# P times V of a sliding-window attention in eight 64x32 array tiles instead of four 128x32 ones

## The chip, the cores and the metric

The kernel runs on one core of a Trainium2 chip. The metric is the time of one execution on the device in microseconds (us); smaller is better. Names of engines in the profile: PE is TensorE's matmul, PEld its weight load, DVE is VectorE, ACT is ScalarE, POOL is GpSimd, SP is SyncE, which here only issues transfers.

## The reference

One transformer block on 2048 tokens of width 640. The normalised input goes through attention (32 heads of 20, causal, each query sees the last 256 keys, itself included) and through a gated feed-forward part of width 1728; both are added to the input.

```python
def _A_ref(x, wqkv, wo):
    H = 32; Dh = D // H; W = 256
    qkv = (x @ wqkv).reshape(B, S, 3, H, Dh).transpose(2, 0, 3, 1, 4)
    q, k, v = qkv[0], qkv[1], qkv[2]
    scores = jnp.einsum("bhqd,bhkd->bhqk", q, k) * (Dh ** -0.5)
    mask = (idx[:, None] - idx[None, :] >= 0) & (idx[:, None] - idx[None, :] < W)
    p = _softmax(jnp.where(mask, scores, -1e9))
    o = jnp.einsum("bhqk,bhkd->bhqd", p, v)
    return o.transpose(0, 2, 1, 3).reshape(B, S, D) @ wo
def _B_ref(x, w_gate, w_up, w_down):
    return (_gelu(x @ w_gate) * (x @ w_up)) @ w_down
xn = _layernorm(x)
return x + _A_ref(xn, A_wqkv, A_wo) + _B_ref(xn, B_w_gate, B_w_up, B_w_down)
```

## The kernel before

There are four stages: normalisation and the first projections (to about 60 us of the profile), attention with dense matmuls as filler (about 60 to 575 us), the rest of the gate and up projections, and the down and output projections. The change lies in the second.

Attention works in units. Unit u is a group g of four heads and a chunk c of 512 queries (u = 4 g + c; 8 groups, 4 chunks, 32 units). For a unit the kernel makes, in this order over time:

- **Max tiles** (`max_pair`, matmuls in L522): scores of 128 queries for two heads against the keys of their window, in array tiles of 60 rows by 64 columns at row 0 or 64; the two heads go to two PSUM banks. VectorE reduces each bank to a maximum per query (L526; one reduction is an instruction and a read of its accumulator). Eight calls a unit make 16 banks. After the last, VectorE negates the maxima (L535, L536).
- **Score tiles** (`exp_piece`, L581): scores again, now keys by queries, one PSUM bank for each of 12 steps. ScalarE takes the exponential into the tile `P` (L583). There are three `P` tiles of 512 columns a unit, X, Z and Y (`pieces`): X holds key blocks b and b-2, Z holds b-1 and b+2, Y holds b+1 and b+3, where b = 4c is the chunk's first key block of 128 keys; a chunk with c = 0 has no earlier blocks. POOL then clears what the mask excludes (`clear`, L594 and L597), block by block in this order.
- **P times V** (`av_unit`, L608): for each piece of a key block (128 keys by n queries) and each of the four heads a matmul in float32, with the head's V (128 keys by 20, and a column of ones whose result is the softmax sum) as a stationary operand of 128 rows by 32 columns. The four heads lie in the four 32-column groups of the array, and all pieces add up in one PSUM bank, `ps_o`. One float32 matmul call shows as two records in the profile, and so does its weight load. ScalarE copies the bank to `ob` (L612), and SyncE's queue stores it (L616, L617).

All of these PSUM banks come from one ring of six (`bank`, L497): each allocation takes the next bank in turn, and its first matmul waits until the last reader of the bank's previous tile is done. Two further banks are for the dense filler.

The order on TensorE, VectorE, ScalarE and POOL is the order in which the program issues the instructions (a schedule written out by hand). `attention` issues a unit in 14 slots. In slot 0 it issues two `max_pair` calls (four banks), then `av_unit` of the unit before, then two more `max_pair` calls, then the first score tile; in slot 2 score tiles 1 to 4; in slots 4 and 8 two `max_pair` calls and two score tiles each; in slot 10 the last three score tiles. At the end of every slot come dense filler matmuls. These names are used below: e0 is the score tile of slot 0, e1 to e4 those of slot 2; max tiles 1 to 4 are the banks filled ahead of P times V in slot 0, and max tiles 5 to 8 those filled behind it.

Three helpers put work off. `defer(n, fn)` calls fn when slot `now + n` takes its list; a slot takes its list at its start, so what is deferred by 0 from within a slot is taken by the next one. `late(fn)` puts fn on a list that `flush` empties near the end of each slot, behind the score tiles; the negation of the maxima goes this way too.

```python
for i in range(NS):
    T = now[0] = NS * u + i
    for fn, a in tick():
        fn(*a)
    if i in BURSTS:
        pull_max(2, T)
    if i == 0 and u:
        av_unit(u - 1)
        flush()
        pull_max(2, T)
    for s in SCORES.get(i, ()) if u < NU else ():
        exp_piece(u, s)
    flush()
```

Of the kernel before, what the change touches and what calls it, by code (L numbers as in the profile page):

```python
# [12 lines left out]
AF = mybir.ActivationFunctionType  # L13
OP = mybir.AluOpType
# [5 lines left out]
C = 512  # L20
# [50 lines left out]
def block_kernel(ctx, tc, x, wqk, wv, wgu, wdo, wdl, out):  # L71
    nc = tc.nc
# [120 lines left out]
    done = set()  # L193
    now = [None]

    def at(slot, fn, *a):
        acts.setdefault(slot, []).append((fn, a))
# [31 lines left out]
    def defer(n, fn, *a):  # L229
        if now[0] is None:  # L230
            fn(*a)
        else:
            at(now[0] + n, fn, *a)
# [190 lines left out]
    with tc.tile_pool(name="lp", bufs=1, side="right") as lp:  # L424
# [5 lines left out]
        ps = psd.tile([128, C], F32, name="ps_u", tag="dn")  # L430
# [48 lines left out]
    vtiles = dict(enumerate(v0[2]))  # L479
# [17 lines left out]
    def bank(name):  # L497
        return psr.tile([128, C], F32, name=name, tag="ring")
# [49 lines left out]
    def pieces(c):  # L548
        b = 4 * c
        X = [(b, 0, 0, 384)] + ([(b - 2, 384, 0, 128)] if c else [])  # L550
        Y = [(b + 1, 0, 128, 384), (b + 3, 384, 384, 128)]
        Z = ([(b - 1, 0, 0, 256)] if c else []) + [(b + 2, 256, 256, 256)]
        return X, Z, Y
# [11 lines left out]
    pts = {}  # L565
# [21 lines left out]
    def clear(u, bi):  # L587
        c = u % NC
        pt = pts[u, bi]
        for p in pieces(c)[bi]:  # L590
            for col, diag in diag_tail(*p, c):
# [4 lines left out]
                else:  # L596
                    nc.gpsimd.affine_select(out=a, in_=a, pattern=[[0, 4], [-1, 128]], compare_op=OP.is_ge,  # L597
                                            fill=0.0, base=-1, channel_multiplier=1)

    def av_unit(u):  # L600
        g, c = divmod(u, NC)
        o, v = bank("ps_o"), vtiles[g]
        todo = [(pts[u, bi], *p) for bi, ps in enumerate(pieces(c)) for p in ps]
        for i, (pt, kb, col, q0, n) in enumerate(todo):
            assert (id(v), kb) in done, (u, kb)
            for j in range(4):
                w0_ = kb * 84 + 21 * j
                nc.tensor.matmul(o[32 * j:32 * j + 32, q0:q0 + n], v[:, w0_:w0_ + 32], pt[:, j, col:col + n],  # L608
                                 start=i == 0, stop=i == len(todo) - 1, skip_group_check=True,
                                 tile_position=(0, 32 * j))  # L610
        ob = ap.tile([128, C], F32, name="ob", tag="ob", bufs=1)
        nc.scalar.activation(ob, o, AF.Copy)  # L612

        def store():
            for j in range(4):
                nc.sync.dma_start(od[c].rearrange("(d h) t -> h d t", h=H)[4 * g + j], ob[32 * j:32 * j + DH, :])  # L616
            nc.sync.dma_start(sd[c][4 * g:4 * g + 4, :], ob[DH::32, :])  # L617

        defer(3, store)
# [184 lines left out]
    def attention():  # L804
# [18 lines left out]
        for u in range(NU + 1):  # L823
# [13 lines that stand above are left out]
                if i in POOL_SLOTS or T < NS:  # L837
                    release(2)
                if u + 3 < NU and i in (KSLOT, 12):
                    load_stack(u + 3, (int(i == KSLOT),))  # L840
                pull_fill(RATE / NS)
# [496 lines left out]
    for j, f in enumerate(range(NFA, NF - 1)):  # L1338
        end = f + 1 == NF - 1
        first, second = {i: [] for i in range(4)}, {i: [] for i in range(4)}  # L1340
# [91 lines left out]
    for n, (p, k) in enumerate(steps):  # L1432
        i = n % (NQD + 1)
        if i == 0:
            begun.clear()
            ps = {b: psn.tile([128, C], F32, name=f"ps_{b}", tag=f"b{b}") for b in (1, 2, 5, 3, 6, 4, 7, 8)}
# [71 lines left out]
```

## Time and profile before

| | us |
|---|---|
| median of 3 runs (1047.58 to 1047.95) | 1047.59 |
| span of the profiled execution, first to last instruction | 1046.8 |
| what lies around the span, against the median | 0.8 |
| TensorE busy (matmul) | 1035.2 |
| VectorE busy | 730.8 |
| ScalarE busy | 513.5 |
| P times V (L608): busy, in 1408 records | 84.3 |
| copy of `ps_o` (L612): 32 copies of 0.597 us | 19.1 |

A row of a group gives line, engine, operation, output and inputs, shapes, count, then busy time in us, the mean of one in ns, and after the second bar the idle time of that engine just before these instructions and what ended it. A row of the timeline gives start and duration in us, and for matmuls also the array tile (rows*columns) and the shape of the moving operand of the first in the run. A row of the windows gives the stretch, its length, the busy time of TensorE, its weight loads, VectorE, ScalarE and POOL with their counts, then the granted clock, the share of the DMA engines and GB/s. Matmuls are pipelined, so the time of a run is read from its start to the start of the next row, not from the durations.

### The profile page before, as it was taken

To read this page: it belongs to the slowest core of one execution; us is meant where nothing else is said; L and a number is where in the kernel's file an instruction comes from. 1 tells how busy PE (TensorE), PEld (TensorE's weight loads), DVE (VectorE), ACT (ScalarE), POOL (GpSimd) and SP (SyncE) were. 2 spreads that over 40 slices of the span, in tenths; PEclk is the share of its full clock that TensorE was granted. 3 is DMA by queue.
4 is the path that set the end of the run, shared out by engine and by line. 5 is a ranking of instruction groups with operands and counts; after the bars stand their busy time and mean duration, and the time that the engine had idled before them with its cause. 6 is when DMAs were issued, how large, how long until landed. Compare 5 with 4: busy or idle time off the path is not lost.

```text
span 1046.8 us, 22733 instructions
## 1 busy us (share of the span) xinstructions
PE 1035.2 (99%) x7997; PEld 827.6 (79%) x7997; DVE 730.8 (70%) x2007; ACT 513.5 (49%) x1088; POOL 333.8 (32%) x503
## 2 busy tenths in 40 slices
PE   8999999999999999999999999999999999999998
PEld 7987666666677766666666888888888999999998
DVE  8745656666665556677662677877655889888887
ACT  4444666765665566656565532223324554333332
POOL 5122667766464458474635111110110000000000
PEclk9999999999999999999999999999999999999999
DMA  5651465545332344444322557677217874443342
GB/s 200 189 150 59 135 183 159 179 148 180 96 117 72 111 145 144 139 130 130 112 79 75 191 189 244 213 251 253 100 61 250 270 241 137 134 128 113 125 134 94
DMA packets 105179, 158.56 MB, mean 151 GB/s; under 512 B 15420, under 2 KB 60092, under 8 KB 105064
## 3 DMA queue, kind: packets, MB, share of 16 engines
q1 hardware_dynamic: 102680, 150.95, 45.0%
q10 hardware_dynamic: 2384, 6.16, 1.9%
q8 instruction: 63, 1.03, 0.4%
q14 instruction: 52, 0.43, 0.1%
HBM read 101.78 MB, written 54.92 MB: 150 GB/s over the span
## 4 chain that ended last, share of the span: by engine, by line
PE 92%; DVE 3%; DMA 2%; ACT 1%; POOL 1%; issue 1%; SPq 0%; DVEq 0%; POOLq 0%; ACTq 0%
PE ps_g L952 21%; PE ps L1219 21%; PE ps_d L110 21%; PE ps_e L581 8%; PE ps_o L608 7%; PE ps_v L110 7%; PE ps_m L522 4%; PE ps_g L110 1%; PE ps_t L181 1%; DVE junk L526 1%; DMA qs<-qd 1%; PE ps_d L356 1%; DVE ss L1057 0%; POOL pt L259 0%; DVE at L1057 0%
## 5 line engine op out<-in xcount | busy, mean ns | idle before, releaser
L526 DVE CUSTOM_DVE_ANT_0 junk<-ps_m,mask 128x320 bf16<-128x320 f32 (+2 forms) x512 | 243.2, 475 | 144.5 <-PE ps_m L522 85.5
L583 ACT ACTIVATE P<-ps_e 128x512 f32<-128x512 f32 (+2 forms) x384 | 195.6, 578 | 60.9 <-PE ps_e L581 59.0
L1219 PE MATMUL ps<-wb,at 128*128 128x320 f32 x999 | 156.0, 309 | 0.0
L1219 PEld LDWEIGHTS ps<-wb,at 128*128 128x128 f32 x999 | 148.9, 188 | 0.3
L594 POOL TENSOR_SCALAR_AFFINE_SELECT P<-P 128x512 f32<-128x512 f32 x128 | 83.9, 657 | 141.0 <-ACT P L583 138.3
L581 PE MATMUL ps_e<-qs,ks 124*128 124x128 bf16 (+2 forms) x704 | 108.0, 277 | 0.7 <-DVE mx L526 0.4
L110 PE MATMUL ps_d<-xh,wqh 128*128 128x512 f32 x350 | 104.4, 410 | 0.0
L110 PE MATMUL ps_d<-xl,wqh 128*128 128x512 f32 x350 | 104.2, 409 | 0.0
L110 PE MATMUL ps_d<-xh,wql 128*128 128x512 f32 x350 | 103.8, 409 | 0.0
L1219 PE MATMUL ps<-wt,at 128*128 128x320 f32 x552 | 89.2, 309 | 0.4 <-DVE u L1057 0.4
L581 PEld LDWEIGHTS <-ks 124*128 124x128 bf16 x704 | 50.8, 98 | 47.8 <-issue 30.1
L608 PE MATMUL ps_o<-P,v 128*32 128x384 f32 (+2 forms) x1408 | 84.3, 386 | 0.6 <-DVE mx L526 0.6
L1219 PEld LDWEIGHTS ps<-wt,at 128*128 128x128 f32 x552 | 82.9, 188 | 0.9 <-DVE u L1057 0.9
L597 POOL TENSOR_SCALAR_AFFINE_SELECT P<-P 128x512 f32<-128x512 f32 x112 | 70.8, 643 | 33.7 <-ACT P L583 33.7
L1173 ACT ACTIVATE at<-ss 128x512 fp32r<-128x512 f32 x59 | 37.3, 632 | 89.6 <-DVE ss L1057 89.6
L103 POOL TENSOR_TENSOR wql<-wr,wqh 128x640 fp32r<-128x640 f32 x11 | 17.6, 1607 | 174.0 <-PE ps_g L952 129.4
L110 PEld LDWEIGHTS ps_d<-xh,wql 128*128 128x128 f32 x350 | 63.9, 189 | 11.1 <-issue 0.3
L608 PEld LDWEIGHTS ps_o<-P,v 128*32 128x32 f32 x1408 | 41.5, 110 | 39.0 <-issue 21.1
L110 PEld LDWEIGHTS ps_d<-xl,wqh 128*128 128x128 f32 x350 | 63.8, 189 | 10.5 <-issue 0.2
L110 PEld LDWEIGHTS ps_d<-xh,wqh 128*128 128x128 f32 x350 | 63.4, 189 | 10.7 <-issue 0.3
L259 POOL TENSOR_TENSOR pt<-r,pt 128x512 bf16<-128x512 f32 x40 | 46.8, 1170 | 67.3 <-ACT pt L258 67.2
L612 ACT ACTIVATE ob<-ps_o 128x512 f32<-128x512 f32 x32 | 19.1, 597 | 86.6 <-PE ps_o L608 72.3
(194 smaller groups left out, 1846.0 us busy)
## 6 DMA issues: line engine op xcount, KB each, us to landing
hr<-hd SPq DMA_DIRECT2D x104, 128.0 KB
hd<-he SPq DMA_DIRECT2D x50, 256.0 KB
wr<-wgu SPq DMA_DIRECT2D x27, 320.0 KB
qs<-qd SPq DMA_DIRECT2D x64, 120.0 KB
ks<-kd SPq DMA_DIRECT2D x64, 120.0 KB
xi<-x SPq DMA_DIRECT2D x16, 320.0 KB
qs<-qd SPq DMA_DIRECT2D x64, 80.0 KB
ks<-kd SPq DMA_DIRECT2D x64, 80.0 KB
```

The costliest lines, as they stand in the source:

```text
L110: nc.tensor.matmul(ps, a(k), b(k), start=n == 0, stop=n == 3 * nk - 1)
L259: nc.gpsimd.tensor_tensor(out=pt[:, l, :], in0=r, in1=pt[:, 1, :], op=OP.subtract)
L522: nc.tensor.matmul(ps[64 * h:64 * h + 64, lo:hi], q[rows, j, q0:q0 + 64], keys, start=True, stop=True, tile_position=(64 * r, 64 * h))
L526: nc.vector.tensor_tensor_reduce(out=junk[:, 0:n], in0=ps[:, 0:n], in1=mask[:, 320 - n:320], scale=1.0, scalar=NEG, op0=OP.add, op1=OP.max ...
L581: nc.tensor.matmul(ps[:, col:col + n], k[0:QROWS, j, kc:kc + 128], q[0:QROWS, j, q0:q0 + n], start=True, stop=True)
L583: nc.scalar.activation(pt[:, j, lo:hi], ps[:, lo:hi], AF.Exp, scale=SCALE)
L594: nc.gpsimd.affine_select(out=a, in_=a, pattern=[[0, 4], [1, 128]], compare_op=OP.is_ge, fill=0.0, base=0, channel_multiplier=-1)
L597: nc.gpsimd.affine_select(out=a, in_=a, pattern=[[0, 4], [-1, 128]], compare_op=OP.is_ge, fill=0.0, base=-1, channel_multiplier=1)
L608: nc.tensor.matmul(o[32 * j:32 * j + 32, q0:q0 + n], v[:, w0_:w0_ + 32], pt[:, j, col:col + n], start=i == 0, stop=i == len(todo) - 1, ski ...
L952: nc.tensor.matmul(ps, i, j, start=first and n == 0, stop=n == len(work) - 1, skip_group_check=True)
L1173: nc.scalar.activation(hi[:, 3:7], s, AF.Copy)
L1219: nc.tensor.matmul(ps[bank][:, 0:HD], *work[bank][j], start=bank not in begun, stop=final[p, bank] == n and j == len(work[bank]) - 1, skip ...
```

## The change

P times V is done in array tiles of 64 rows by 32 columns: every key block is cut into two halves of 64 keys (h = 0 and 1), in array rows 0 to 63 and 64 to 127. A half of 64 keys is seen by 320 queries at most, where the whole block of 128 is seen by 384, so the stream over a half is shorter. The two halves add up in two PSUM banks, `halves[0]` and `halves[1]`, both allocated at the start of `av_unit`. The halves are paired so that both of a pair have the same number of queries; `windows` gives for each pair the key blocks and columns, and its order is that of blocks (b, b), (b+3, b-2), (b-2, b+3), (b+2, b-1), (b-1, b+2), (b+1, b+1). A chunk with c = 0 takes b, b+1, b+2, b+3, and its first pair has 320 and 384 queries. ScalarE copies `halves[0]` to `ob`; VectorE adds `halves[1]` to `ob` in an instruction that is issued through `defer(0, late, ...)`. The stores are as before, three slots after P times V.

```diff
+    def windows(c):
+        r = {}
+        for bi, ps in enumerate(pieces(c)):
+            for kb, col, q0, n in ps:
+                for h in range(2):
+                    first = 128 * (kb - 4 * c) + 64 * h
+                    lo = max(0, first) if kb else 0
+                    hi = min(C, first + 320)
+                    r[h, kb - 4 * c] = bi, kb, col + lo - q0, lo, hi - lo
+        pairs = [((0, 0), (1, 0)), ((0, 3), (1, -2)), ((0, -2), (1, 3)), ((0, 2), (1, -1)), ((0, -1), (1, 2)),
+                 ((0, 1), (1, 1))]
+        if not c:
+            pairs = [((0, d), (1, d)) for d in range(4)]
+        return [[(h, *r[h, d]) for h, d in p] for p in pairs]
+
     def av_unit(u):
         g, c = divmod(u, NC)
-        o, v = bank("ps_o"), vtiles[g]
-        todo = [(pts[u, bi], *p) for bi, ps in enumerate(pieces(c)) for p in ps]
-        for i, (pt, kb, col, q0, n) in enumerate(todo):
-            assert (id(v), kb) in done, (u, kb)
+        halves, v = [bank("ps_o") for _ in range(2)], vtiles[g]
+        todo = windows(c)
+        for i, pair in enumerate(todo):
             for j in range(4):
-                w0_ = kb * 84 + 21 * j
-                nc.tensor.matmul(o[32 * j:32 * j + 32, q0:q0 + n], v[:, w0_:w0_ + 32], pt[:, j, col:col + n],
-                                 start=i == 0, stop=i == len(todo) - 1, skip_group_check=True,
-                                 tile_position=(0, 32 * j))
+                for h, bi, kb, col, q0, n in pair:
+                    assert (id(v), kb) in done, (u, kb)
+                    rows, w0_ = slice(64 * h, 64 * h + 64), kb * 84 + 21 * j
+                    nc.tensor.matmul(halves[h][32 * j:32 * j + 32, q0:q0 + n], v[rows, w0_:w0_ + 32],
+                                     pts[u, bi][rows, j, col:col + n], start=i == 0, stop=i == len(todo) - 1,
+                                     skip_group_check=True, tile_position=(64 * h, 32 * j))
         ob = ap.tile([128, C], F32, name="ob", tag="ob", bufs=1)
-        nc.scalar.activation(ob, o, AF.Copy)
+        nc.scalar.activation(ob, halves[0], AF.Copy)
+        defer(0, late, lambda: nc.vector.tensor_tensor(out=ob, in0=halves[1], in1=ob, op=OP.add))
```

## The prediction

> **What bounds the kernel now.** I read the page first, busy times and chain, then a window over the stretch in which the changed code runs (95 to 575 us), then the groups of its instructions, and last the timeline of one unit, engine by engine.
>
> ```profile
> span 1046.8 us, 22733 instructions
> ...
> PE 1035.2 (99%) x7997; PEld 827.6 (79%) x7997; DVE 730.8 (70%) x2007; ACT 513.5 (49%) x1088; POOL 333.8 (32%) x503
> ...
> PE 92%; DVE 3%; DMA 2%; ACT 1%; POOL 1%; issue 1%; SPq 0%; DVEq 0%; POOLq 0%; ACTq 0%
> ```
> ```profile
> 95.00:575.00 480.00, 476.70 (x4710) 319.21 (x4709) 298.37 (x1106) 295.92 (x645) 280.55 (x440) 1.00 0.42 127
> ```
>
> TensorE is the bound: 92% of the chain, and in the attention stretch 476.7 of 480 us busy, at a granted clock of 1.00. Its order is written out, so a microsecond taken from its stream is a microsecond gained, and a microsecond for which its next instruction waits is lost. Only 3.3 us of idle time exist there that a delay could hide in. So I ask two things: how much shorter the stream of P times V gets, and whether anything behind it comes to wait.
>
> Here are the groups of P times V and of the score tiles, then one unit with c above 0 (c is the query chunk): TensorE, VectorE, ScalarE.
>
> ```profile
> L608 PE MATMUL ps_o<-P,v 128*32 128x384 f32 x512 | 53.8, 492 | 0.6 <-DVE mx L526 0.6
> L608 PE MATMUL ps_o<-P,v 128*32 128x256 f32 x448 | 30.1, 379 | 0.0
> L608 PE MATMUL ps_o<-P,v 128*32 128x128 f32 x448 | 22.5, 273 | 0.0
> L522 PE MATMUL ps_m<-ks,qs 60*64 60x320 bf16 x512 | 30.5, 308 | 0.7 <-ACT ob L612 0.7
> L522 PE MATMUL ps_m<-ks,qs 60*64 60x64 bf16 x288 | 22.3, 200 | 1.4 <-DVE r L273 0.7 <-DMA qs<-qd 0.6
> ```
> ```profile
> 301.28 2.80 PE L608 MATMUL ps_o<-P,v 128*32 128x384 f32 x48
> 304.00 0.47 PE L522 MATMUL ps_m<-ks,qs 60*64 60x320 bf16 x8
> 304.40 0.39 PE L581 MATMUL ps_e<-qs,ks 124*128 124x128 bf16 x2
> ...
> 305.67 1.05 PE L581 MATMUL ps_e<-qs,ks 124*128 124x128 bf16 x8
> ```
> ```profile
> 301.25 0.49 DVE L526 CUSTOM_DVE_ANT_0 junk<-ps_m,mask 128x320 bf16<-128x320 f32 x1 [2.30 <-PE ps_m L522]
> ...
> 303.60 0.08 DVE L526 DVE_READ_ACCUMULATOR2_ANT mx<- 128x1 f32 x1
> 304.38 0.49 DVE L526 CUSTOM_DVE_ANT_0 junk<-ps_m,mask 128x320 bf16<-128x320 f32 x1 [0.70 <-PE ps_m L522]
> ...
> 306.73 0.08 DVE L526 DVE_READ_ACCUMULATOR2_ANT mx<- 128x1 f32 x1
> 306.85 0.17 DVE L535 TENSOR_SCALAR nm<-mx 128x16 bf16<-128x16 f32 x1
> 307.06 0.17 DVE L536 SCALAR_TENSOR_TENSOR nm<-mx,nm 128x16 bf16<-128x16 f32 x1
> ```
> ```profile
> 304.14 0.60 ACT L612 ACTIVATE ob<-ps_o 128x512 f32<-128x512 f32 x1 [2.83 <-PE ps_o L608]
> ```
>
> The unit runs like this. Four max tiles are in PSUM when P times V starts at 301.28, and VectorE reduces them beside it (four reductions, 301.25 to 303.68, 0.645 us apart). At 304.00 TensorE writes four more, at 304.40 the first score tile e0, then dense filler, and at 305.67 the next four score tiles, e1 to e4. VectorE reduces the second four from 304.38 to 306.81 and negates the maxima until 307.23. Nothing on TensorE waits: the ring of six banks just suffices. Counting allocations in program order (max tiles 1 to 4, ps_o, max tiles 5 to 8, e0, e1), e0 takes the bank of max tile 4, read by 303.68, and e1 takes the bank of ps_o, copied by 304.74.
>
> **The shorter stream.** One call becomes two matmul records (24 calls in a unit with c above 0, 48 records at 301.28). From 128 to 256 columns a record grows from 273 to 379 ns, 0.828 ns a column, so a call costs 1.656 ns a column, and its four array tiles run side by side: 1536 columns give 2.54 us, and 304.00 minus 301.28 is 2.72, so 0.18 us is entry and exit. After the change the six pairs have 320, 128, 64, 256, 192 and 320 columns, 1280 in all: 2.12 + 0.18 = 2.30, a gain of 0.42 us. In a chunk with c = 0 it is 384 + 320 + 256 + 128 = 1088 in place of 1152 columns: 0.11 us. With 24 and 8 units: 11.0 us.
>
> This supposes that the two row halves run side by side as the four column tiles do. No fp32 row halves are in the trace; the nearest row is the one at 304.00. Its eight 320-column matmuls take 0.40 us to the next row. By the L522 records a column costs (308 - 200)/256 = 0.42 ns, so one at a time they would need 1.08 us and two at a time 0.54. More than two run at once, so row halves do overlap there, in two banks. I take the full gain; the bounds are full overlap and one half after the other (a rival below).
>
> The records double (96 matmuls and as many weight loads a unit); I price that at nothing, since weight loads run beside matmuls and the 16 short max matmuls below are issued within 0.41 us; if it were not so, the gain of 0.42 would shrink toward nothing, which goes into the range.
>
> ```profile
> 300.87 0.47 PE L522 MATMUL ps_m<-ks,qs 60*64 60x64 bf16 x16
> ```
>
> **The second bank.** The change takes two banks of the ring in place of one, so every successor moves: max tiles 5 to 8 take the banks of max tiles 1 to 4, e0 takes the bank that ScalarE copies, and e1 takes the bank that VectorE adds. The Trainium skill, TensorEngine Tiling (Array Packing), section Gotcha 1: PSUM Pressure, says that different row tiles must write different banks and that row tiling raises the pressure on PSUM; it speaks against this change, gives no price, and the rows below supply one.
>
> First, e0. It would arrive at 304.40 - 0.42 = 303.98. The copy would run from 304.14 - 0.42 = 303.72 to 304.32. So TensorE waits there about 0.4 us.
>
> Second, e1. The added VectorE instruction is deferred with delay 0 from a slot whose calls have been taken already, so it is issued in the next slot, behind the second four reductions and the negation, and still before e1 to e4. It has the form of these rows (128x512 f32, one operand in PSUM):
>
> ```profile
> L273 DVE TENSOR_TENSOR r<-ps_d,pt 128x512 f32<-128x512 f32 x30 | 20.6, 688 | 17.5 <-ACT pt L277 13.3 <-POOL pt L259 4.0 <-ACT mr L545 0.2
> L669 DVE TENSOR_TENSOR gs<-ps_d,gs 128x512 f32<-128x512 f32 x16 | 11.0, 688 | 12.7 <-PE ps_d L110 12.7
> ```
>
> The max tiles come 0.42 earlier, so the reductions do too (the first four are done at 303.68, in time for 303.96). The second negation starts at 307.06 - 0.42 = 306.64, the next instruction 0.09 later (291.86 and 291.95 in the rows below), the add ends at 306.73 + 0.69 = 307.42, and with 0.05 us for the signal (an estimate; VectorE waits 0.04 on itself between 306.81 and 306.85) e1 starts at 307.47. Before it was 305.67. The unit gets 1.80 us longer, the gain of 0.42 and the wait at e0 included. All that TensorE has queued behind e1 moves with it.
>
> In a unit with c = 0:
>
> ```profile
> 286.63 2.15 PE L608 MATMUL ps_o<-P,v 128*32 128x384 f32 x32
> 288.71 0.47 PE L522 MATMUL ps_m<-ks,qs 60*64 60x320 bf16 x8
> ...
> 290.50 1.05 PE L581 MATMUL ps_e<-qs,ks 124*128 124x128 bf16 x8
> ```
> ```profile
> 286.61 0.49 DVE L526 CUSTOM_DVE_ANT_0 junk<-ps_m,mask 128x320 bf16<-128x320 f32 x1 [1.11 <-PE ps_m L522]
> ...
> 289.19 0.49 DVE L526 CUSTOM_DVE_ANT_0 junk<-ps_m,mask 128x320 bf16<-128x320 f32 x1
> ...
> 291.86 0.17 DVE L536 SCALAR_TENSOR_TENSOR nm<-mx,nm 128x16 bf16<-128x16 f32 x1
> 291.95 0.68 DVE L661 SCALAR_TENSOR_TENSOR he<-he,gs 128x512 f32<-128x512 f32 x1
> ```
>
> Here VectorE runs from 286.61 to 292.03 with no wait, so a shorter P times V moves nothing: the add goes where L661 stands, 291.95 to 292.64, and e1 starts at 292.69 in place of 290.50, 2.19 later.
>
> Of 32 units the last two have no max tiles behind them: one loses 0.14 + 0.60 + 0.05 - 0.42 = 0.37 at e0, one gains 0.42, together nothing. The other 30 are 22 with c above 0 and 8 with c = 0: 22 x 1.80 + 8 x 2.19 = 57.1 us.
>
> **The new order of the key blocks.** The second pair now reads the last key block of the chunk, whose mask POOL applies last; before, it came last. Units 13 and 26:
>
> ```profile
> 301.00 0.63 POOL L594 TENSOR_SCALAR_AFFINE_SELECT P<-P 128x512 f32<-128x512 f32 x1
> ```
> ```profile
> 495.74 2.80 PE L608 MATMUL ps_o<-P,v 128*32 128x384 f32 x48
> ...
> 496.49 0.63 POOL L594 TENSOR_SCALAR_AFFINE_SELECT P<-P 128x512 f32<-128x512 f32 x1
> ```
>
> The second pair is due 320 x 1.656 = 0.53 us after the start. In the one unit the mask is done at 301.63, before 301.81, and costs nothing; in the other it is done at 497.12 and due at 496.27, 0.85 us late. The bounds for 24 units are 0 and 20 us. I take 0.25 each, 6 us, nearer to the first, since each unit also gets 1.8 us longer, in which POOL catches up. The stores of `ob` come two slots behind the add and hold nothing that TensorE waits for: nothing.
>
> **Sum.** 57 + 6 - 1 (some of the 3.3 us of idle time absorbs a little) = 62 us. The profiled span of 1046.8 becomes 1108.8; the median of the runs, 1047.59, is 0.8 above the span, so 1109.6 us.
>
> **The rivals.**
>
> *Faster.* If the ring left e0 and e1 banks that are free, only the stream counts: 1047.6 - 11 + 6 = 1042.6. It decides at one point, whether both copies end before 303.98 and 305.25. For it: VectorE is idle 2.3 us before 301.25. Against it: the idle time lies ahead of P times V, not behind, and the trace has a successor of ps_o that waits for its copy (L522 <-ACT ob, 0.7 us). Chance 0.04.
>
> *The add is not late.* If VectorE added right behind the copy, at 304.32 + 0.69 = 305.01, e1 would be due at 305.67 - 0.42 + 0.39 = 305.64 and find its bank free. Left are the waits at e0: 22 x (0.39 - 0.42) + 8 x (0.39 - 0.11) = 1.6, with POOL's 6 about 1055. The same page of the Trainium skill, section PSUM Bottleneck, advises to use both ScalarE and VectorE for emptying PSUM, which would give this time. Against it stands the queue: four reductions and two negations are issued between the end of P times V and the add. Chance 0.05.
>
> *The row halves take turns.* Then 1280 columns cost twice, 4.24 us, 2.12 more than forecast in 24 units; with c = 0 1.80 more, of which VectorE's own run hides some 0.2, so 1.6 in 8; and POOL's wait is nearly hidden (-5): 1110 + 51 + 13 - 5, about 1168. For it: no fp32 row halves in the trace. Against it: the row at 304.00. Chance 0.10.
>
> **How the numbers follow.** The forecast has 0.80, and 0.01 is for what I don't see. The range is the forecast's own: below, POOL at 0 (-6), all idle time used (-2), and e1 a quarter of a microsecond sooner in 30 units (-8), 1093; above, POOL at 20 (+14) and no gain from the eight tiles (+11), 1135. It leaves out the rivals, 0.2. Faster by over 0.2% (about what a measurement of this kernel can tell from no change) is the first rival and a little: 0.05; within 0.2%: 0.01; slower: 0.94.
>
> **What would show it.** In the profile after, P times V to the next max tile takes 2.3 us (right) or over 4 (row halves in turn); L581 on TensorE shows idle time whose releaser is VectorE, near 1.8 us a unit; TensorE's busy time falls by some 10 us while the span grows; the add starts right behind L536. Were TensorE's idle time in the stretch still near 3 us, the forecast would be wrong at the bank of e1.

## The result, and the profile after

The changed kernel takes 1067.32 us (median of 4 runs, 1066.96 to 1068.45), beside it the kernel before 1047.77 (4 runs, 1047.58 to 1048.11). The ratio is 1.0185, interval 1.0171 to 1.02. It is slower, as predicted, but by 19.5 us where 62 had been forecast, and lies below the range.

From the page of the changed kernel: span, busy times, and the shares of the chain.

```profile
span 1065.3 us, 25671 instructions
...
PE 1039.4 (98%) x9405; PEld 840.3 (79%) x9405; DVE 751.1 (71%) x2039; ACT 514.1 (48%) x1088; POOL 334.1 (31%) x503
...
PE 79%; DMA 4%; POOL 4%; DVE 4%; ACT 4%; SPq 2%; issue 2%; DVEq 0%; POOLq 0%; ACTq 0%
```

TensorE is still busy 98% of the span, but the chain now passes through POOL, VectorE and ScalarE with 4% each. The waits of the changed kernel say who stopped TensorE (engine, instruction, releaser: us in total, times, longest), first for its matmuls and then for its weight loads:

```profile
PE ps_e L581 <- ACT ob L628: 6.0, 21, 0.3
PE ps_o L624 <- POOL P L594: 5.3, 10, 1.3
PE ps_o L624 <- POOL P L597: 2.2, 1, 2.2
...
PE ps_m L522 <- DVE ob L629: 0.7, 2, 0.5
```
```profile
PEld ps_o L624 <- POOL P L594: 17.2, 23, 1.9
PEld ps_o L624 <- POOL P L597: 3.6, 2, 2.9
```

The row on which the forecast stood, L581 waiting for VectorE's add (L629), is not there. What is there is L581 waiting for ScalarE's copy, about 0.3 us at a time, 21 times, and P times V waiting for POOL's masks. Unit 13 again on the timeline of the changed kernel, TensorE, then VectorE, then ScalarE (start, duration, idle time before):

```profile
308.22 0.77 PE L624 MATMUL ps_o<-P,v 64*32 64x320 f32 x16
309.19 2.02 PE L624 MATMUL ps_o<-P,v 64*32 64x128 f32 x80 [0.21 <-POOL P L594]
311.14 0.47 PE L522 MATMUL ps_m<-ks,qs 60*64 60x320 bf16 x8
311.88 0.38 PE L581 MATMUL ps_e<-qs,ks 124*128 124x128 bf16 x2 [0.27 <-ACT ob L628]
...
313.12 1.05 PE L581 MATMUL ps_e<-qs,ks 124*128 124x128 bf16 x8
```
```profile
314.19 0.17 DVE L536 SCALAR_TENSOR_TENSOR nm<-mx,nm 128x16 bf16<-128x16 f32 x1
314.46 0.69 DVE L629 TENSOR_TENSOR ob<-ps_o,ob 128x512 f32<-128x512 f32 x1
```
```profile
311.23 0.60 ACT L628 ACTIVATE ob<-ps_o 128x512 f32<-128x512 f32 x1 [2.98 <-PE ps_o L624]
```

Three things are to be seen. e0 starts at 311.88, 0.05 us after the copy ended at 311.83; it is 0.74 behind the max tiles where it was 0.40. The add starts at 314.46, behind L536, and takes 0.69, as forecast. But e1 started at 313.12, before the add had even begun: e1 does not use the bank that VectorE reads.

The difference splits up as follows, from the row starts of all 32 units in the two profiled runs. From the start of the first P times V to the end of the last one it is 17.2 us more:

| us, all units | before | after | difference |
|---|---|---|---|
| start of P times V to next row | 82.07 | 88.40 | +6.3 |
| next row to e0 | 13.25 | 22.81 | +9.6 |
| e0 to e1 | 41.39 | 41.12 | -0.3 |
| the rest of the units | | | +1.6 |

Behind it follow 1.3 us more in the later stages and 0.9 more around the span (1067.04 for the profiled run, against a span of 1065.3).

The first row is itself a sum. A unit with c above 0 that waits for no mask takes 2.48 us (430.63 to 433.12) in place of 2.72, and one with c = 0 takes 1.88 (292.45 to 294.33) in place of 2.08. Undisturbed, the 32 units would take 24 x 2.48 + 8 x 1.88 = 74.6, 7.5 less than before; the other 13.8 are waits, by the rows above mainly for POOL.

```profile
430.63 2.55 PE L624 MATMUL ps_o<-P,v 64*32 64x320 f32 x96
433.12 0.47 PE L522 MATMUL ps_m<-ks,qs 60*64 60x320 bf16 x8
```
```profile
292.45 1.95 PE L624 MATMUL ps_o<-P,v 64*32 64x320 f32 x64
294.33 0.91 PE L522 MATMUL ps_m<-ks,qs 60*64 60x320 bf16 x8
```

### The profile page after: what moved, and what is told of

It is laid out like the page before. It is cut to its first block, busy times and chain, and to the rows that moved or that the text cites. A ratio compares the mean times of both kernels' runs of the same rounds, so it can differ in the third digit from the quotient of the medians.

```text
span 1065.3 us, 25671 instructions
## 1 busy us (share of the span) xinstructions
PE 1039.4 (98%) x9405; PEld 840.3 (79%) x9405; DVE 751.1 (71%) x2039; ACT 514.1 (48%) x1088; POOL 334.1 (31%) x503
## 4 chain that ended last, share of the span: by engine, by line
PE 79%; DMA 4%; POOL 4%; DVE 4%; ACT 4%; SPq 2%; issue 2%; DVEq 0%; POOLq 0%; ACTq 0%
PE ps_g L969 21%; PE ps L1236 19%; PE ps_d L110 17%; PE ps_e L581 7%; PE ps_v L110 6%; PE ps_o L624 4%; PE ps_m L522 3%; ACT P L583 1%; POOL P L594 1%; DMA qs<-qd 1%; PE ps_g L110 1%; ACT ob L628 1%; DVE junk L526 1%; SPq L493 1%; POOL P L597 1%
## 5 line engine op out<-in xcount | busy, mean ns | idle before, releaser
L594 POOL TENSOR_SCALAR_AFFINE_SELECT P<-P 128x512 f32<-128x512 f32 x128 | 83.6, 655 | 149.0 <-ACT P L583 148.7
L581 PE MATMUL ps_e<-qs,ks 124*128 124x128 bf16 (+2 forms) x704 | 107.7, 277 | 8.1 <-ACT ob L628 6.0
L581 PEld LDWEIGHTS <-ks 124*128 124x128 bf16 x704 | 52.2, 98 | 53.0 <-issue 35.6
L624 PE MATMUL ps_o<-P,v 64*32 64x320 f32 (+5 forms) x2816 | 83.1, 351 | 8.1 <-POOL P L594 5.3
L624 PEld LDWEIGHTS ps_o<-P,v 64*32 64x32 f32 x2816 | 50.4, 106 | 28.8 <-POOL P L594 17.2
L522 PEld LDWEIGHTS <-qs 60*64 60x64 bf16 x1472 | 27.4, 105 | 48.9 <-issue 45.5
```

The lines of the kernel that those rows point to most:

```text
L522: nc.tensor.matmul(ps[64 * h:64 * h + 64, lo:hi], q[rows, j, q0:q0 + 64], keys, start=True, stop=True, tile_position=(64 * r, 64 * h))
L581: nc.tensor.matmul(ps[:, col:col + n], k[0:QROWS, j, kc:kc + 128], q[0:QROWS, j, q0:q0 + n], start=True, stop=True)
L594: nc.gpsimd.affine_select(out=a, in_=a, pattern=[[0, 4], [1, 128]], compare_op=OP.is_ge, fill=0.0, base=0, channel_multiplier=-1)
L624: nc.tensor.matmul(halves[h][32 * j:32 * j + 32, q0:q0 + n], v[rows, w0_:w0_ + 32], pts[u, bi][rows, j, col:col + n], start=i == 0, stop=i ...
```

## The experiments

The first question was why e1 did not wait. In the bank addresses of the compiled changed kernel, e1 has the bank of max tile 5, in each of the 30 units with max tiles behind P times V, and in unit 13 the bank of `halves[1]` goes to a max tile of slot 4, thirteen allocations later. So, other than the description of the kernel before has it, the ring does not hand its banks on strictly in turn: the bank of a late reader goes to a later tile. By which rule it chooses is open. The expectation below takes the order in which the last readers are issued. That is not quite it: in unit 13 the banks of e1 and e2 are handed on ahead of that of `halves[1]`, though the add is issued before their exponentials. Theory 1: the forecast's price for e1 was right, and only this order took it away. The rival: the price was wrong too. Four runs came first.

**rot_after: the changed kernel with a ring that takes banks strictly in turn.** The same ring put into the kernel before is the control, **rot_before**.

```diff
+    turns = [0]
     def bank(name):
-        return psr.tile([128, C], F32, name=name, tag="ring")
+        turns[0] += 1
+        return psr.tile([128, C], F32, name=name, tag=f"ring{turns[0] % 6}", bufs=1)
```

> The changed kernel with the ring made strict: six banks taken in turn, whatever was released first. Theory 1 (the forecast's wait at e1 was right in price, and failed only because a bank is handed on in the order in which its readers are issued, so that the added bank goes to a max tile of slot 4 and not to e1): with the strict ring e1 takes the bank that VectorE adds, the add of the shown unit ends at 315.15 and e1 stood at 313.12, so about 2.1 us a unit in 30 units, 62 us, less some of POOL's 13.8 us of waits that fit into the longer units: 1110 to 1130 us, and L581 on TensorE shows 45 to 65 us of idle time released by VectorE's add. Theory 2 (the price was wrong: TensorE would not stand at that wait for long, whichever bank e1 takes): 1067 to 1075 us.

> The kernel before with the same strict ring, to price the strict ring itself. Both theories: its banks come nearly in turn already, so 1047 to 1053 us.

The changed kernel with the strict ring took 1132.99 us (1129.4 to 1134.45; 4 runs), a ratio of 1.0798 (1.0773 to 1.0822) to the kernel before, here 1048.65. The control took 1049.53, ratio 1.0013 (1.0004 to 1.0022). So the strict ring by itself costs about 1 us, and with two banks 66 us more than the changed kernel had. The waits, and one unit on TensorE and VectorE (the added lines move every line number by 3: L584 is the score tiles, L632 the add):

```profile
PE ps_e L584 <- DVE ob L632: 59.1, 30, 2.5
PE ps_o L627 <- POOL P L597: 5.5, 9, 1.5
```
```profile
337.41 2.55 PE L627 MATMUL ps_o<-P,v 64*32 64x320 f32 x96
339.90 0.47 PE L525 MATMUL ps_m<-ks,qs 60*64 60x320 bf16 x8
340.63 0.38 PE L584 MATMUL ps_e<-qs,ks 124*128 124x128 bf16 x2 [0.27 <-ACT ob L631]
...
343.97 1.05 PE L584 MATMUL ps_e<-qs,ks 124*128 124x128 bf16 x8 [1.93 <-DVE ob L632]
```
```profile
342.94 0.18 DVE L539 SCALAR_TENSOR_TENSOR nm<-mx,nm 128x16 bf16<-128x16 f32 x1
343.22 0.69 DVE L632 TENSOR_TENSOR ob<-ps_o,ob 128x512 f32<-128x512 f32 x1
```

This is the unit that the prediction described: the add behind the second negation, ended at 343.91, and e1 at 343.97. The wait is there in exactly 30 units, 1.97 us each. From the start of P times V to e1 the unit takes 6.56 us (337.41 to 343.97) in place of 4.39 (301.28 to 305.67): 2.17 longer, where 1.80 had been worked out. So the missing term of the forecast is shown: with banks taken in turn the wait comes, in this unit at a price a fifth above the forecast's, and the order in which banks are handed on had removed it. The time is above the expectation. The waits for POOL shrank only by some 3 us in the longer units (P times V sums to 85.52 us here, to 88.40 in the changed kernel). The granted clock was 0.995 in the profiled run (1129.4 us) and 0.992 to 0.989 in the other three (1131.66 to 1134.45); what that adds was not measured by itself.

**order: the changed kernel, with the pairs in the order in which POOL finishes the masks**, and the 64-column pair last.

```diff
-        pairs = [((0, 0), (1, 0)), ((0, 3), (1, -2)), ((0, -2), (1, 3)), ((0, 2), (1, -1)), ((0, -1), (1, 2)),
-                 ((0, 1), (1, 1))]
+        pairs = [((0, 0), (1, 0)), ((0, 2), (1, -1)), ((0, -1), (1, 2)), ((0, 1), (1, 1)), ((0, 3), (1, -2)),
+                 ((0, -2), (1, 3))]
         if not c:
-            pairs = [((0, d), (1, d)) for d in range(4)]
+            pairs = [((0, d), (1, d)) for d in (0, 2, 1, 3)]
```

> The changed kernel with the key blocks in another order: the pairs with tile Y, whose mask POOL applies last, come last (and the pair of 64 queries at the very end). Theory 1 (P times V waits for POOL's mask because the change moved the last block to second place, 13.8 us in all over the undisturbed 2.48 and 1.88 us a unit): with the masks where they are now, due 1.27 and 1.80 us after the start, about 2 us of these waits are left, so 1054 to 1057 us, and the idle time of L624 released by POOL falls from over 15 us to under 4. Theory 2 (P times V is longer for another reason, as the doubled number of instructions): 1064 to 1068 us.

It took 1055.79 us (1054.58 to 1056.38), ratio 1.0065 (1.005 to 1.008): 11.5 us less than the changed kernel, as theory 1 expected. Its waits (matmuls, then weight loads) and unit 13:

```profile
PE ps_e L581 <- ACT ob L628: 6.3, 20, 0.3
...
PE ps_o L624 <- POOL P L594: 0.9, 1, 0.9
```
```profile
PEld ps_o L624 <- POOL P L594: 2.8, 4, 1.6
```
```profile
304.62 2.45 PE L624 MATMUL ps_o<-P,v 64*32 64x320 f32 x96
307.00 0.47 PE L522 MATMUL ps_m<-ks,qs 60*64 60x320 bf16 x8
307.77 0.38 PE L581 MATMUL ps_e<-qs,ks 124*128 124x128 bf16 x2 [0.31 <-ACT ob L628]
```

The weight loads' wait for L594 falls from 17.2 us to 2.8. The P times V stretches sum to 75.99 us in place of 88.40, that is 12.4 less: 10.0 of masks (13.8 to 3.8), and 2.4 because an undisturbed unit now takes 2.38 us, not 2.48. About half of what is left of the waits is one unit, number 24, where POOL's queue stood 5.93 us behind a store of its buffer `tx`:

```profile
466.68 0.74 POOL L756 TENSOR_TENSOR tx<-xh 128x256 f32<-128x256 f32 x1 [5.93 <-DMA td<-tx]
```

**e0late: the changed kernel with e0 moved from slot 0 to slot 1**, behind the dense filler of slot 0, so that the copy has time. As a control the same edit was made in the kernel before, **e0late_before**.

```diff
-SCORES = {0: range(0, 1), 2: range(1, 5), 4: range(5, 7), 8: range(7, 9), 10: range(9, 12)}
+SCORES = {1: range(0, 1), 2: range(1, 5), 4: range(5, 7), 8: range(7, 9), 10: range(9, 12)}
```

> The changed kernel with the first score tile e0 issued in slot 1 in place of slot 0, behind a slot's dense filler, so that ScalarE's copy has freed its bank. Theory 1 (0.34 us a unit of wait at e0 for the copy, 9.6 us in all): 1056 to 1060 us, and the idle time of L581 released by the copy goes to nothing. Theory 2 (the wait moves on to e1 to e4, since ScalarE's exponential of e0 comes later and their banks with it): 1064 to 1068 us.

> The kernel before, with e0 issued in slot 1 as in the run where that brought the changed kernel only 1 us. Theory 1 (there the wait for the copy was gone, and its place was taken by one more change between dense filler and score tile, 0.2 us a unit, since e0 no longer stands next to the max tiles): here, with no wait to save, 5 to 8 us slower, 1053 to 1056 us. Theory 2 (the wait moved on through the banks of e1 to e4): no such cost in the kernel before, 1047 to 1049 us.

e0late took 1066.15 us (1065.25 to 1066.61; ratio 1.0163, 1.0146 to 1.018), only 1.2 below the changed kernel. Theory 1, that the whole wait of about 10 us would come back, failed as it stood. The wait on the copy did go: no row of it is left among TensorE's waits. But a new row grew among the weight loads, from 2.5 us in 9 places in the changed kernel to this in e0late:

```profile
PEld ps_d L110 <- issue: 7.4, 27, 0.5
```

The control shows the price of it without any second bank: 1053.89 us (1053.22 to 1056.7), ratio 1.006 (1.0047 to 1.0074), 6 us slower than the kernel before. The same row, before and in the control:

```profile
PEld ps_d L110 <- issue: 0.8, 4, 0.3
```
```profile
PEld ps_d L110 <- issue: 7.2, 30, 0.3
```

A score tile in the middle of the dense filler makes TensorE change once more between the two kinds of tiles in each of 30 units. The weight loads of the filler stand 0.24 us for it where nothing is awaited, and the kernel becomes 0.2 us a unit longer. With 9.6 us saved and 6 paid, `e0late` should have gained 3.6; it gained 1.2, and the other 2.4 are not accounted for. The Trainium skill, TensorEngine Tiling (Array Packing), Key Properties, says that a change of tiling mode, not merely of tile, drains TensorE; it gives no price. The score tiles and the filler may both have all 128 rows and columns as far as the profile's 124*128 and 128*128 tell, so whether this is that drain is not shown here. The price is.

For the next three runs `order` is the base.

**shortcopy: ScalarE copies only 256 of 512 columns of `halves[0]`.** VectorE adds to those and copies the other 256 columns of `halves[1]`; half of the sums of the first bank are left out.

```diff
-        nc.scalar.activation(ob, halves[0], AF.Copy)
-        defer(0, late, lambda: nc.vector.tensor_tensor(out=ob, in0=halves[1], in1=ob, op=OP.add))
+        nc.scalar.activation(ob[:, 0:256], halves[0][:, 0:256], AF.Copy)
+        def add():
+            nc.vector.tensor_tensor(out=ob[:, 0:256], in0=halves[1][:, 0:256], in1=ob[:, 0:256], op=OP.add)
+            nc.vector.tensor_copy(ob[:, 256:512], halves[1][:, 256:512])
+        defer(0, late, add)
```

> The kernel with the new order of key blocks (1055.8 us), with ScalarE copying only 256 of the 512 columns of the first bank; VectorE adds these and copies the other 256 of the second bank, so half of the first bank's sums is left out of the result. Theory 1 (e0 waits for ScalarE's copy of its bank, 0.38 us a unit): the copy gets about 0.2 us shorter, so does the wait, 30 units, 6 us: 1049 to 1051 us. Theory 2 (e0 is late for another reason, as the array's change from P times V to scores): 1055 to 1057 us.

The runs spread over 5 us: 1055.32 us (1052.22 to 1057.37), ratio 1.0066 (1.0049 to 1.0084). That decides nothing about the time. The profiled run, the shortest of the four, shows the mechanism: e0 starts 0.56 us after the max tiles (304.84 to 305.40), not 0.77, right behind the shorter copy, which ends at 305.36. Over all units the time from the max tiles to e0 sums to 19.14 us, 5.1 less than in `order` (24.21), near the 6 of theory 1. Four of the eight units with c = 0 (8, 12, 16 and 28) keep their 0.84 us, so there it isn't the copy that holds e0. In these, max tiles 5 to 8, which now take the banks of max tiles 1 to 4, wait for VectorE's reductions: in unit 12 of the changed kernel their row lasts 0.91 us (at 294.33 above), in the kernel before 0.47.

```profile
304.84 0.47 PE L522 MATMUL ps_m<-ks,qs 60*64 60x320 bf16 x8
305.40 0.38 PE L581 MATMUL ps_e<-qs,ks 124*128 124x128 bf16 x2
```

**wide64: the pair of 64 queries widened to 128**, which adds products with masked zeros and nothing else.

```diff
                     lo = max(0, first) if kb else 0
                     hi = min(C, first + 320)
+                    if hi - lo == 64 and c:
+                        lo, hi = (lo, hi + 64) if h == 0 else (lo - 64, hi)
```

> The kernel with the new order of key blocks, with the pair of 64 queries widened to 128 (the added products are with entries that the mask has set to zero, so the sums are the same). Theory 1 (a round of eight 64-column matmuls takes as long as its sixteen instructions need, not as its columns): P times V stays within 0.04 us of the 2.38 us of a unit with c above 0, and the time within 1 us of 1055.8. Theory 2 (the columns set the time there too): 64 more columns at 1.656 ns, 0.11 us a unit, 2.48 us, and 2.5 us more in all, 1058 us.

It took 1058.84 us (1058.19 to 1061.69), ratio 1.0112 (1.0096 to 1.0127). Unit 13 takes 2.48 us (305.12 to 307.60), 0.10 more than in `order`, which is 64 columns at 1.656 ns. Theory 1, that a short round costs as much as a longer one because its instructions can't be issued faster, is wrong for that pair at the end of the order; theory 2, columns alone, is right there.

```profile
305.12 2.55 PE L626 MATMUL ps_o<-P,v 64*32 64x320 f32 x96
307.60 0.47 PE L522 MATMUL ps_m<-ks,qs 60*64 60x320 bf16 x8
```

**split: one of the two max calls behind P times V moved to slot 2**, ahead of e1 to e4.

```diff
                 if i == 0 and u:
                     av_unit(u - 1)
                     flush()
-                    pull_max(2, T)
+                    pull_max(1, T)
+                if i == 2 and u:
+                    pull_max(1, T - 2)
```

> The kernel with the new order of key blocks, with one of the two max calls behind P times V moved to slot 2, right ahead of e1: e0 then takes the bank of max tile 3, long free, and max tile 8 the bank that ScalarE copies. Theory 1 (the wait at e0 is all that is left between the two kernels but for a few waits of POOL): the 11 us of it go, and nothing else comes late (VectorE needs max tile 7 at 1.8 us behind P times V and gets it at about 2.2, and e4 takes the added bank, whose add then runs behind two reductions in place of four): 1044 to 1047 us, at or below the kernel before. Theory 2 (the later reductions and the added bank at e4 make a new wait): 1050 to 1056 us.

This changes the number of allocations between `halves[0]` and e0, and it lets the add pass two reductions. It took 1047.76 us (1045.9 to 1050.44; 11 runs) against 1047.92 (1047.48 to 1049.15; 15 runs); the ratio is 0.9996 (0.9987 to 1.0005), no difference. The unit on TensorE, and ScalarE's copy:

```profile
301.29 2.45 PE L624 MATMUL ps_o<-P,v 64*32 64x320 f32 x96
303.67 0.33 PE L522 MATMUL ps_m<-ks,qs 60*64 60x320 bf16 x4
303.93 0.39 PE L581 MATMUL ps_e<-qs,ks 124*128 124x128 bf16 x2
...
305.28 0.33 PE L522 MATMUL ps_m<-ks,qs 60*64 60x320 bf16 x4
305.54 1.05 PE L581 MATMUL ps_e<-qs,ks 124*128 124x128 bf16 x8
```
```profile
303.80 0.60 ACT L628 ACTIVATE ob<-ps_o 128x512 f32<-128x512 f32 x1 [2.47 <-PE ps_o L624]
```

e0 starts at 303.93, while the copy still runs (303.80 to 304.40): it no longer has the copied bank, and the wait is gone. With the wait at e0 out of the way, and most of those for POOL, the eight tiles bring what they have: P times V sums to 74.96 us, 7.1 below the kernel before. 5.3 of it are given back between P times V and e1 (59.95 against 54.64 us in all), where the max call now stands alone among the filler: one more change between kinds of tiles in a unit, and 0.18 us of 30 units is about the price that `e0late_before` showed. That this is its cause was not tested by itself. So even the best arrangement tried here only equals the kernel before.

## Why the prediction was right or wrong

**The step that failed** is in "The second bank": that each allocation takes the next bank in turn, so that "e1 takes the bank that VectorE adds". I read the ring as a counter. In this kernel the bank of a late reader goes to a later tile, and e1 took the bank of max tile 5. So the wait at e1, which carried nearly all of the forecast 62 us, never came. The waits of the kernel before held a sign of it, which I even quoted, as evidence against "faster":

```profile
PE ps_m L522 <- ACT ob L612: 0.7, 2, 0.3
```

Here a max tile waits for the copy of `ps_o`. Six banks taken in turn always give that bank to e1, six allocations on, and never to a max tile; with the strict ring of `rot_before` the row is gone.

`rot_after` shows that the rest of the step held: the place of the add behind L536, its 0.69 us, the 0.05 for the signal (0.06), and 30 units. The price was low by 0.37 us in the shown unit: 0.18 because the stream was longer than forecast, and 0.19 because the add starts 0.28 us after L536 (342.94 to 343.22) and not 0.09. That the change is slower was thus forecast mainly by a wait that did not come. What makes it slower are 13.8 us of waits within P times V, mainly for POOL, and 9.6 ahead of e0, against 7.5 gained. I had listed the ring's slack as a rival ("faster", e0 and e1 both free), but with a test on when the copies end, not on which bank goes to whom. Half of that rival came true, at e1.

**e0** was right with c above 0: it gets the copied bank, and the wait is 0.34 us (0.74 less 0.40) where 0.39 had been worked out. With c = 0 e0 comes 0.39 to 0.44 later, but in the four units named under `shortcopy` the cause is another. The prediction had VectorE run there "with no wait" and priced nothing for max tiles 5 to 8, which now wait for its reductions. In all e0 costs 9.6 us more; 1.3 us for which a max tile had waited before, in units 2 and 9, are already taken off.

**The shorter stream** was mis-sized. The gain of a unit is 0.24 us with c above 0, not 0.42, and 0.20 with c = 0, not 0.11; together 7.5, not 11.0. The price of a column was right, by the groups of the changed kernel:

```profile
L624 PE MATMUL ps_o<-P,v 64*32 64x320 f32 x960 | 53.5, 435 | 2.8 <-POOL P L597 2.2 <-DVE mx L526 0.6
L624 PE MATMUL ps_o<-P,v 64*32 64x128 f32 x448 | 14.9, 278 | 5.3 <-POOL P L594 5.3
```

From 128 to 320 columns a record grows by 157 ns, 0.82 ns a column, as before. Row halves do run side by side, so that rival fell. With c = 0 the pairs are unequal (320 and 384 columns, twice 320, 256 and 192, 128 and 64), and I had added up the longer half of each, 1088 columns. The sum of the half that streams more is 320 + 320 + 256 + 128 = 1024 columns, and 1.70 + 0.18 = 1.88 us is what was measured. The starts of the single records in unit 12 agree: the tiles with 320 columns reach the next pair at 0.56 us, those with 384 beside them at 0.67, so the halves do not wait for each other. With c above 0 what is lost are about 0.18 us that don't grow with columns. 0.10 of it goes when the 64-column pair comes last (`order`, 2.38). In the starts of the single records of the changed kernel, the eight tiles leave the 64-column round out of step, one about 0.1 us ahead of the rest in every later round. That this causes the loss is argued, not shown. The remaining 0.08 us are open.

**The order of the key blocks** was mis-sized: 13.8 us of waits, inside the bounds of 0 and 20, where I took 6. Unit 26 came as worked out (0.89 us late against 0.85). Unit 13, priced at nothing, lost 0.44 (2.92 less 2.48). The reason for taking the low side was wrong as well. I had thought that POOL would catch up in longer units, but in the 2 us longer units of `rot_after` it hardly did, 10.9 of the 13.8 us stayed: POOL's masks wait for ScalarE's exponentials of the same unit, and these move along with TensorE. The changed kernel's POOL in unit 26:

```profile
508.51 1.18 POOL L594 TENSOR_SCALAR_AFFINE_SELECT P<-P 128x512 f32<-128x512 f32 x1 [1.37 <-ACT P L583]
```

**The rivals.** "The add is not late" gave 1055 for waits at e0 alone with POOL's 6. Its mechanism did not happen, since the add was late; but its state of TensorE did. Its sum with the measured terms, 1055 + 7.8 (POOL) + 3.5 (stream), is 1066.3, beside the measured 1067.3. The Trainium skill, TensorEngine Tiling (Array Packing), PSUM Bottleneck, advises to empty PSUM with both ScalarE and VectorE. The time neither bears that out nor refutes it: VectorE's share cost TensorE 0.7 us in the changed kernel and 59.1 us in `rot_after`, by the order of banks alone. Gotcha 1: PSUM Pressure of the same page of the Trainium skill says that row tiling raises the pressure on PSUM. The 9.6 us ahead of e0 bear it out.

**The signs.** P times V to the next max tile near 2.3 us: nearly. L581 idle with VectorE as releaser: absent, and ScalarE in its place, which named the failed step at once. TensorE's busy time to fall by some 10 us: it rose by 4.2. Why is open; the profile models the ends of matmuls.

## What to carry to other kernels

Before pricing a wait for a buffer, find out which buffer the waiting instruction gets. The ring of this kernel, which does not hand its banks on in turn, punished a late reader far less than one taken in turn (1067 against 1133 us), and one call moved can take a wait away (`split`). And when work is regrouped for a shorter stream, keep its inputs in the order in which the engine before finishes them: here the new order alone cost more (11.5 us came back with `order`) than the shorter stream gained (7.5).

## What the runs showed of the hardware that was not expected

- One more change between a score tile and dense filler cost about 0.2 us, with nothing awaited: 6 us over 30 units in `e0late_before`. Moving an instruction to a place where its data are ready isn't free if it breaks up a run of one kind.
- Eight fp32 tiles of 64x32 keep the price of a column of four tiles of 128x32 (0.82 and 0.83 ns in each record), so row halves with twice the weight loads stream at full rate, and halves of unequal length do not wait for each other. But a short round in the middle cost 0.10 us that the same round at the end did not.
